# Two capacities swap ranks, the block sums change engine, and the next group's norm is taken one layer earlier

## The chip, the cores and the metric

The kernel runs on one core of a Trainium2 chip. The metric is the device time of one execution in microseconds (us). Its engines are named as the profile does: PE is TensorE (matmul) and PEld its weight load, DVE is VectorE, ACT is ScalarE, POOL is GpSimd, SP is the queue of SyncE that issues most DMA transfers.

## What is computed

Three blocks follow one another on 4608 tokens (8 batches of 576) of width 512:

```
scores = q k^T / 8 within chunks of 64 positions; attn = softmax(scores); x = attn v
e(t) = argmax of x[t] w_gate        (8 experts);  p(t) = its softmax probability
x[t] = p(t) * relu(x[t] w1[e]) w2[e]              (512 -> 1024 -> 512)
h = x w_in                                        (512 -> 2048)
g = h where h >= 1;  0 where h <= -1;  (h + 1)^2 / 4 between
out = g w_out                                     (2048 -> 512)
```

All inputs are float32 (w_in and w_out of the last block may be wider), drawn from a fixed seed. The sizes of the experts are thus data of the run: how many tokens choose each expert.

## The kernel before, in words

Every operand of a product is scaled by a power of two and split into a float16 high and a float16 low part (`high` on ScalarE, `low` on VectorE), and a product is three float16 products: high-high, high-low, low-high.

**Attention** runs over 36 tiles of 128 tokens. Behind it the tokens of each expert are listed in DRAM. **The expert stage** goes through eight slots r = 0 to 7. `RANKS[r]` says which expert a slot takes: the one of that rank when the experts are sorted by their number of tokens. Slot 0 is an exception: it takes the expert that has most tokens in the first 12 tiles, found early so that its weights can be loaded (`rank_first`), and this expert counts as rank 0 in the sorting (line 687). `CAPS[r]` is the number of tokens that slot r has room for; a slot over 512 is worked in two windows, of 384 and of the rest (line 743). Slot 2 has rank 1.

Tokens beyond a slot's capacity go through **the overflow loop** (`overflow`, lines 938 to 1069), a loop on the device whose number of trips is computed from the counts (`overflow_plan`: the tokens over each capacity in blocks of 128, and one more term that is zero unless slot 0 was misjudged). One trip loads the expert's weights again, scales and splits them, works 128 tokens, stores them, and then prepares the rows of group 0 of the next stage again (`again`).

**The last MLP** goes through nine groups of 512 tokens. Both layers are one level of Strassen-like block products: seven products in place of eight, on sums and differences of blocks. `rows_of(g)` prepares the first layer's operand: four loads from the expert outputs `yts` into `xf` by SP; eight squares with row sums on ScalarE, whose outputs go into the operand buffer `xt2` as junk; a maximum over the partitions on GpSimd (`allmax`, line 372); the power-of-two scale (`pow2`) on VectorE; four block differences (`B_SUMS`) on GpSimd (line 1168); then the high and low parts into `xt2`, and constants of the group (`mlp_consts`). `first_layer` (line 1218) makes for each of four column blocks jj seven products into PSUM (line 1232), sums between them (`add`, helper line 345), the activation (`gate`: ScalarE line 1242, VectorE lines 1247 and 1248, helper line 348), the splits of four operands (`split`: ScalarE line 1190, VectorE helper line 345), and four block sums S1 to S4 on GpSimd (line 1271) with their splits. `second_layer` (line 1276) makes seven products on these operands (line 1283), copies between PSUM banks (`copy`, line 1213), and scatters the output rows from GpSimd's queue (line 392).

**The order of the work** is written by a planner in the kernel (`Plan.order`): each operation is a task with an estimated duration (`cost`), tasks get due times backwards from TensorE's order, and an engine takes, of the tasks that are ready, the one due first. Each engine then executes its queue strictly in that order. For the last stage (`plan.beside`) the planner lengthens VectorE operations with two inputs in SBUF by 1.4 (tensor_tensor) or 1.22. In the trace the helpers' operations have the helper's line: 345 (`both`), 348 (`fused`), 375 (`square`), 378 (`high`), 381 (`low`).

Of the kernel before, what the change touches and what calls it, by code (L numbers as in the profile page):

```python
# [30 lines left out]
CAPS = (704, 512, 672, 480, 640, 448, 640, 672)  # L31
# [26 lines left out]
    KB * n for n in (0, 16, 32, 48, 76, 86, 92, 100, 108, 124, 131, 135, 179, 193, 201))  # L58
YS = [KB * n for n in (124, 126, 128, 193, 195, 197, 199)]
# [30 lines left out]
class Plan:  # L90
# [6 lines left out]
    def __init__(self, joined):  # L97
        self.tasks, self.writer, self.readers, self.joiners = [], {}, {}, {}
        self.clock, self.last = 0.0, None
        self.seen, self.joined, self.rows, self.beside, self.chains, self.links, self.direct = None, joined, set(), False, {}, set(), False  # L100
# [30 lines left out]
    def cost(self, engine, op, out, a, k):  # L131
# [12 lines left out]
        if engine == "DVE":  # L144
# [4 lines left out]
            if self.beside and n >= 256 and op != "tensor_scalar":  # L149
                apart = [v.space for v in [k.get(i) for i in ("in0", "in1")] if v is not None]  # L150
                if PSUM not in apart and len(apart) == 2:
                    t *= 1.4 if op == "tensor_tensor" else 1.22
# [141 lines left out]
def build(ctx, tc, qT, kT, v1, wg, w1, w2, wi, wo, out):  # L294
# [859 lines left out]
    def rows_of(g, eng):  # L1154
# [5 lines left out]
        for n in range(8):  # L1160
            t, c = n // 4, n % 4 * 64
            square(ss[:, n:n + 1], xf[:, 2 * t:2 * t + 2, :, c:c + 64], xt2[:, t, 0:2, :, c:c + 64].bitcast(BF16))
# [3 lines left out]
        for c0, c1 in (0, 1), (1, 2), (2, 3), (3, 4), (4, 5), (5, 7):  # L1166
            for o, x, y in {2: B_SUMS[:1], 3: B_SUMS[1:2], 4: B_SUMS[2:3], 5: B_SUMS[3:]}.get(c0, ()):
                do(lambda o=o, x=x, y=y: eng.tensor_tensor(out=xf[:, o], in0=xf[:, x], in1=xf[:, y], op=ALU.subtract))  # L1168
# [3 lines left out]
        mlp_consts(i_y, sets[g % 2])  # L1172
# [45 lines left out]
    def first_layer(g, ci):  # L1218
# [31 lines left out]
        for jj in range(4):  # L1250
# [19 lines left out]
            for o, a, b, f in (S1, A21, A22, ALU.add), (S2, S1, A11, ALU.subtract), (S3, A11, A21, ALU.subtract), (S4, A12, S2, ALU.subtract):  # L1270
                do(lambda o=o, a=a, b=b, f=f, jj=jj: pool.tensor_tensor(out=o.raw(jj), in0=a.raw(jj), in1=b.raw(jj), op=f))  # L1271
# [83 lines left out]
    for r in range(E):  # L1355
# [6 lines left out]
        while w < len(windows) and windows[w][0] == r:  # L1362
# [13 lines left out]
            if w == len(windows) - 2:  # L1376
# [3 lines left out]
                plan.beside = True  # L1380
                rows_of(0, pool)
                plan.beside = False
# [11 lines left out]
    overflow(lambda: rows_of(0, pool), [xf, xt2] + list(sets[0].values()))  # L1394

    plan.beside = True
    for g in range(NG):
        ci = sets[g % 2]
        first_layer(g, ci)
        if g + 1 < NG:  # L1400
            rows_of(g + 1, pool)
        second_layer(g, ci["io"])
# [59 lines left out]
```

## Time and profile before

| | |
|---|---|
| median of 3 timed runs | 1469.31 us (1461.74 to 1470.01) |
| profiled execution | 1454.82 us, of which the span from first to last instruction is 1453.1 us |
| mean granted TensorE clock | 0.939 |
| HBM read, written | 178.04 MB, 43.95 MB |

The timed runs and the profiled one are different executions. Busy time is the time in which an engine executes; "idle before" is the gap ahead of an instruction, with what ended it. An arrow out<-in names the buffers written and read; nearly all of SBUF is one tile, `arena`, and all PSUM banks are `psum`.

### The profile page before, as it was taken

To read this page: it belongs to the slowest core of one execution; us is meant where nothing else is said; L and a number is where in the kernel's file an instruction comes from. 1 tells how busy PE (TensorE), PEld (TensorE's weight loads), DVE (VectorE), ACT (ScalarE), POOL (GpSimd) and SP (SyncE) were. 2 spreads that over 40 slices of the span, in tenths; PEclk is the share of its full clock that TensorE was granted. 3 is DMA by queue.
4 is the path that set the end of the run, shared out by engine and by line. 5 is a ranking of instruction groups with operands and counts; after the bars stand their busy time and mean duration, and the time that the engine had idled before them with its cause. 6 is when DMAs were issued, how large, how long until landed. Compare 5 with 4: busy or idle time off the path is not lost.

```text
span 1453.1 us, 27496 instructions
## 1 busy us (share of the span) xinstructions
PE 1254.1 (86%) x10617; PEld 982.0 (68%) x10617; DVE 1035.7 (71%) x1977; ACT 852.3 (59%) x1550; POOL 513.8 (35%) x449
## 2 busy tenths in 40 slices
PE   6999695999999998532798998898998989899997
PEld 5777454557466575422687777787887778788776
DVE  5667477887787884222695968879595977969593
ACT  3444567887988883323564737565464736556462
POOL 3023143177211111110271625445261624527053
PEclk9999788999999999755899999999999999999998
DMA  9999558889989889231433517061442507053220
GB/s 231 288 259 250 165 201 198 271 226 288 271 216 252 273 242 310 97 66 37 135 98 104 159 32 216 15 218 45 136 127 75 187 2 233 29 159 103 91 92 30
DMA packets 149845, 233.50 MB, mean 161 GB/s; under 512 B 58111, under 2 KB 89343, under 8 KB 147665
## 3 DMA queue, kind: packets, MB, share of 16 engines
q1 hardware_dynamic: 139776, 207.95, 48.5%
q0 software_dynamic: 9936, 23.79, 5.8%
q8 instruction: 83, 1.36, 0.4%
q14 instruction: 50, 0.40, 0.1%
HBM read 178.04 MB, written 43.95 MB: 153 GB/s over the span
## 4 chain that ended last, share of the span: by engine, by line
PE 40%; DVE 29%; DMA 10%; issue 8%; ACT 7%; POOL 5%; SPq 1%; POOLq 0%; DVEq 0%; ACTq 0%
DVE arena L348 12%; DVE arena L345 12%; PE psum L1283 10%; PE psum L886 9%; PE psum L902 9%; PE psum L1232 6%; DMA arena<-arena 3%; POOL arena L1271 2%; DVE psum L345 2%; DMA arena<-kT 2%; PE psum L575 2%; PE psum L561 1%; PE psum L555 1%; DVE arena L381 1%; DMA yt<-arena 1%
## 5 line engine op out<-in xcount | busy, mean ns | idle before, releaser
L1232 PE MATMUL psum<-arena 128*128 128x256 f16 x3024 | 339.8, 273 | 58.1 <-DVE cells L345 28.3
L1283 PE MATMUL psum<-arena 128*128 128x256 f16 x3024 | 353.3, 279 | 30.1 <-ACT psum L1213 26.4
L1232 PEld LDWEIGHTS <-arena 128*128 128x128 f16 x3024 | 296.3, 98 | 98.7 <-issue 64.2
L1283 PEld LDWEIGHTS <-arena 128*128 128x128 f16 x3024 | 302.3, 100 | 75.4 <-issue 27.8
L1271 POOL TENSOR_TENSOR arena<-arena 128x512 f32<-128x512 f32 x144 | 229.4, 1608 | 191.6 <-DVE arena L348 172.6
L345 DVE TENSOR_TENSOR arena<-arena 128x512 f16<-128x512 f32 (+5 forms) x301 | 266.8, 915 | 15.9 <-ACT arena L1190 13.9
L1190 ACT ACTIVATE arena<-arena 128x512 f16<-128x512 f32 x252 | 154.6, 627 | 124.3 <-DVE arena L345 56.6
L886 PE MATMUL psum<-arena 128*128 128x384 f16 (+6 forms) x1248 | 205.1, 327 | 20.6 <-DMA arena<-arena 14.6
L381 DVE SCALAR_TENSOR_TENSOR arena<-arena,cells 128x1024 f16<-128x1024 f32 (+2 forms) x186 | 190.6, 1062 | 29.0 <-ACT arena L378 27.2
L378 ACT ACTIVATE arena<-arena,cells 128x1024 f16<-128x1024 f32 (+2 forms) x186 | 168.8, 960 | 65.0 <-DVE cells L342 37.4
L902 PE MATMUL psum<-arena 128*128 128x384 f16 (+6 forms) x1248 | 198.2, 319 | 2.9 <-ACT arena L891 1.0
L886 PEld LDWEIGHTS <-arena 128*128 128x128 f16 x1248 | 124.8, 100 | 97.7 <-issue 23.6
L348 DVE SCALAR_TENSOR_TENSOR arena<-psum,cells,arena 128x512 f32<-128x512 f32 x171 | 125.4, 747 | 81.0 <-PE psum L1283 43.4
L902 PEld LDWEIGHTS <-arena 128*128 128x128 f16 x1248 | 121.8, 98 | 76.3 <-issue 2.7
L348 DVE SCALAR_TENSOR_TENSOR arena<-arena,cells 128x512 f32<-128x512 f32 x108 | 132.4, 1232 | 44.3 <-ACT arena L1242 44.1
L1242 ACT ACTIVATE arena<-psum,cells 128x512 f32<-128x512 f32 x144 | 107.4, 771 | 40.8 <-DVE psum L345 20.1
L375 ACT ACTIVATE arena<-arena 128x1024 bf16<-128x1024 f32 (+1 forms) x160 | 115.7, 727 | 10.0 <-DMA arena<-yt 7.5
L392 POOL DMA_INDIRECT out<-arena,sid x36 | 40.6, 1128 | 186.7 <-DVE arena L348 150.5
L372 POOL PARTITION_ALL_REDUCE cells<-cells x47 | 21.4, 456 | 235.2 <-DVE cells L351 157.8
L392 POOL DMA_INDIRECT ld<-arena x36 | 35.1, 974 | 119.1 <-DVE arena L612 50.1
L1168 POOL TENSOR_TENSOR arena<-arena 128x512 f32<-128x512 f32 x40 | 63.6, 1598 | 33.9 <-issue 16.5
L892 DVE SCALAR_TENSOR_TENSOR arena<-psum,arena 128x384 f16<-128x384 f32 (+6 forms) x104 | 54.8, 536 | 27.8 <-ACT arena L891 27.4
(189 smaller groups left out, 1165.6 us busy)
## 6 DMA issues: line engine op xcount, KB each, us to landing
arena<-wd SPq DMA_DIRECT2D x252, 256.0 KB, 3.1
arena<-w SPq DMA_DIRECT2D x64, 512.0 KB, 7.3
arena<-yt SPq DMA_DIRECT2D x40, 256.0 KB, 4.8
arena<-v SPq DMA_DIRECT2D x36, 260.0 KB, 7.3
xd<-arena SPq DMA_DIRECT2D x18, 512.0 KB, 7.3
arena<-qT SPq DMA_DIRECT2D x16, 512.0 KB, 11.1
arena<-kT SPq DMA_DIRECT2D x32, 256.0 KB, 8.5
arena<-w_in SPq DMA_DIRECT2D x8, 1024.0 KB, 5.5
```

The source lines that it names most:

```text
L345: do(lambda: dve.tensor_tensor(out=out, in0=a, in1=b, op=op))
L348: do(lambda: dve.scalar_tensor_tensor(out=out, in0=a, scalar=s, in1=b, op0=op, op1=op1))
L375: do(lambda: act.activation(out=junk, in_=src, func=AF.Square, scale=scale, accum_out=ss))
L378: do(lambda: act.activation(out=hi, in_=src, func=AF.Copy, scale=s))
L381: do(lambda: dve.scalar_tensor_tensor(out=lo, in0=src, scalar=s, in1=hi, op0=ALU.mult, op1=ALU.subtract))
L886: pe.matmul(h[:, 0:n], lhsT=wa[:, a, wc:wc + P], rhs=xt[:, 4 * b + dc, 0:n], start=dc == 0 and i == 0, stop=dc == 3 and i == 2)
L902: pe.matmul(ybanks[db][:, 0:n], lhsT=wb[:, b, f * D + db * P:f * D + db * P + P], rhs=ht[:, a, f, 0:n], start=f == 0 and i == 0, stop=f == ...
L1190: do(lambda: act.activation(out=self.parts(0, jj), in_=self.raw(jj), func=AF.Copy))
L1232: pe.matmul(banks[to][:, k], lhsT=w[:, k, x, dc * P:(dc + 1) * P], rhs=xt2[:, z, b, dc], start=start and (k, dc, m) == (0, 0, 0), stop=(k, ...
L1242: do(lambda: act.activation(out=r, in_=at[src], func=AF.Relu, scale=a, bias=b))
L1271: do(lambda o=o, a=a, b=b, f=f, jj=jj: pool.tensor_tensor(out=o.raw(jj), in0=a.raw(jj), in1=b.raw(jj), op=f))
L1283: pe.matmul(banks[to][:, i], lhsT=a.part(x, j, i * P, P), rhs=wot[b][:, j, v], start=start and (j, i, n) == (0, 0, 0), stop=(j, i, n) == ( ...
```

## The change

The capacities of slots 0 and 2 are exchanged. The four block differences of `rows_of` and the four block sums of `first_layer` are issued on VectorE (`both`) in place of GpSimd. `rows_of` becomes two functions: `load_rows` has the loads, squares, maximum, scale, differences and constants, `split_rows` the high and low parts. For group g + 1 the first is called ahead of group g's first layer, the second stays between the layers. The squares' outputs go to a buffer of their own (`junk`). The planner's lengthening for work beside GpSimd is removed.

```diff
--- before.py
+++ after.py
@@ -28,7 +28,7 @@
 BIG = 1 << 20
 LC = NT + 4
 RANKS = (0, 5, 1, 6, 3, 7, 4, 2)
-CAPS = (704, 512, 672, 480, 640, 448, 640, 672)
+CAPS = (672, 512, 704, 480, 640, 448, 640, 672)
 WIDE = 384
 BATCH = (6, 6, 6, 4, 6, 5, 3)
 GB = max(BATCH)
@@ -56,6 +56,7 @@
 KB = 1024
 WT0, WT1, WT2, RAWS, XG, XH, XT0, XT1, HT, Y, NU, STAGE, RINGS, FREE, END = (
     KB * n for n in (0, 16, 32, 48, 76, 86, 92, 100, 108, 124, 131, 135, 179, 193, 201))
+JUNK = 134 * KB
 YS = [KB * n for n in (124, 126, 128, 193, 195, 197, 199)]
 XF, XT = 135 * KB, 149 * KB
 OPS = [KB * n for n in (0, 72, 82, 32, 92, 102, 112)]
@@ -97,7 +98,7 @@
     def __init__(self, joined):
         self.tasks, self.writer, self.readers, self.joiners = [], {}, {}, {}
         self.clock, self.last = 0.0, None
-        self.seen, self.joined, self.rows, self.beside, self.chains, self.links, self.direct = None, joined, set(), False, {}, set(), False
+        self.seen, self.joined, self.rows, self.chains, self.links, self.direct = None, joined, set(), {}, set(), False
 
     def keys(self, ap):
 
@@ -146,10 +147,6 @@
                 return 0.1 + 0.0003 * n
             t = max(0.15, 0.12 + (0.0006 if op == "tensor_scalar" and n > 64 and out.space != PSUM else 0.00112) * n)
             t += 0.05 * (op == "scalar_tensor_tensor" and n > 64)
-            if self.beside and n >= 256 and op != "tensor_scalar":
-                apart = [v.space for v in [k.get(i) for i in ("in0", "in1")] if v is not None]
-                if PSUM not in apart and len(apart) == 2:
-                    t *= 1.4 if op == "tensor_tensor" else 1.22
             return t
         if engine == "POOL":
             return {"indirect_dma_start": 1.27, "partition_all_reduce": 0.4, "tensor_tensor": 0.2 + 0.0027 * n}.get(op, 0.4)
@@ -1151,7 +1148,9 @@
     xt2 = view(XT, (2, 7, 2, HD), F16)
     wot = [view(a, (8, 2, HD), F16) for a in WOT]
 
-    def rows_of(g, eng):
+    junk = [view(JUNK + 512 * i, (2, 2, 64), BF16) for i in range(2)]
+
+    def load_rows(g):
 
         for db in range(4):
             dh, dc = divmod(db, 2)
@@ -1159,17 +1158,20 @@
         ss, am, ag = cell(8), cell(), cell()
         for n in range(8):
             t, c = n // 4, n % 4 * 64
-            square(ss[:, n:n + 1], xf[:, 2 * t:2 * t + 2, :, c:c + 64], xt2[:, t, 0:2, :, c:c + 64].bitcast(BF16))
+            square(ss[:, n:n + 1], xf[:, 2 * t:2 * t + 2, :, c:c + 64], junk[n % 2])
         reduce(am, ss, ALU.max)
         allmax(ag, am)
         s, i_y = pow2(ag, TY, 1, True)
-        for c0, c1 in (0, 1), (1, 2), (2, 3), (3, 4), (4, 5), (5, 7):
-            for o, x, y in {2: B_SUMS[:1], 3: B_SUMS[1:2], 4: B_SUMS[2:3], 5: B_SUMS[3:]}.get(c0, ()):
-                do(lambda o=o, x=x, y=y: eng.tensor_tensor(out=xf[:, o], in0=xf[:, x], in1=xf[:, y], op=ALU.subtract))
+        for o, x, y in B_SUMS:
+            both(xf[:, o], xf[:, x], xf[:, y], ALU.subtract)
+        mlp_consts(i_y, sets[g % 2])
+        return s
+
+    def split_rows(s):
+
         for c0, c1 in (0, 2), (3, 4), (4, 5), (2, 3), (5, 7):
             high(xt2[:, 0, c0:c1], xf[:, c0:c1], s)
             low(xt2[:, 1, c0:c1], xt2[:, 0, c0:c1], xf[:, c0:c1], s)
-        mlp_consts(i_y, sets[g % 2])
 
     class Operand:
 
@@ -1268,7 +1270,7 @@
             gate(z, A21, jj, 1)
             A22.split(jj)
             for o, a, b, f in (S1, A21, A22, ALU.add), (S2, S1, A11, ALU.subtract), (S3, A11, A21, ALU.subtract), (S4, A12, S2, ALU.subtract):
-                do(lambda o=o, a=a, b=b, f=f, jj=jj: pool.tensor_tensor(out=o.raw(jj), in0=a.raw(jj), in1=b.raw(jj), op=f))
+                both(o.raw(jj), a.raw(jj), b.raw(jj), f)
             A12.split(jj)
             for o in S2, S1, S3, S4:
                 o.split(jj)
@@ -1377,9 +1379,7 @@
                 for n in (0, 6, 1, 5, 4, 2, 3):
                     for j in 0, 4:
                         do(lambda n=n, j=j: sp.dma_start(out=wot[n][:, j:j + 4].rearrange("p a x c -> p (a x c)"), in_=wdo[n][:, j:j + 4].rearrange("p j c -> p (j c)")))
-                plan.beside = True
-                rows_of(0, pool)
-                plan.beside = False
+                split_rows(load_rows(0))
                 for n in range(RING):
                     fetch_unit(n)
             gt = cell()
@@ -1391,14 +1391,14 @@
             if w == 2:
                 overflow_plan()
             w += 1
-    overflow(lambda: rows_of(0, pool), [xf, xt2] + list(sets[0].values()))
-
-    plan.beside = True
+    overflow(lambda: split_rows(load_rows(0)), [xf, xt2] + junk + list(sets[0].values()))
+
     for g in range(NG):
         ci = sets[g % 2]
+        s = load_rows(g + 1) if g + 1 < NG else None
         first_layer(g, ci)
         if g + 1 < NG:
-            rows_of(g + 1, pool)
+            split_rows(s)
         second_layer(g, ci["io"])
 
     E_ = mybir.EngineType
```

## Rows read from the trace of the kernel before

**Rows 1.** The page, part 1: busy time and share of the span by engine.
```profile
PE 1254.1 (86%) x10617; PEld 982.0 (68%) x10617; DVE 1035.7 (71%) x1977; ACT 852.3 (59%) x1550; POOL 513.8 (35%) x449
```

**Rows 2.** Busy time by stretch: from:to, length, engines, PE clock, DMA share, GB/s.
```profile
0.00:603.80 603.80, 548.52 (x4377) 365.45 (x4377) 428.11 (x1099) 400.69 (x737) 172.43 (x213) 0.96 0.83 239
603.80:698.60 94.80, 21.00 (x193) 17.92 (x192) 24.61 (x67) 30.49 (x61) 15.90 (x16) 0.56 0.23 63
866.30:948.20 81.90, 74.39 (x675) 65.67 (x674) 65.28 (x93) 47.65 (x87) 36.96 (x25) 1.00 0.38 117
```

**Rows 3.** Timeline around the overflow loop (start, length, instruction, idle before), and one group.
```profile
593.95 0.23 DVE L983 TENSOR_SCALAR loop<-csum,jt 128x10 f32<-128x10 f32 x1 [0.59 <-DVE arena L892]
603.52 0.38 PE L898 MATMUL psum<-arena 128*128 128x512 f16 x1
...
L1052 PE MATMUL psum<-arena 128*128 128x128 f16 x96 | 11.5, 308 | 34.8 <-DMA arena<-arena 29.9 <-DVE arena L1055 4.8
...
698.61 26.35 PE L1232 MATMUL psum<-arena 128*128 128x256 f16 x228 [28.29 <-DVE cells L345]
```

**Rows 4.** Timeline of TensorE alone in the last MLP's groups.
```profile
768.55 12.96 PE L1283 MATMUL psum<-arena 128*128 128x256 f16 x102 [3.64 <-ACT psum L1213]
903.98 2.78 PE L1232 MATMUL psum<-arena 128*128 128x256 f16 x24 [1.71 <-DVE psum L345]
935.08 11.29 PE L1283 MATMUL psum<-arena 128*128 128x256 f16 x102 [3.19 <-ACT psum L1213]
1350.72 14.16 PE L1283 MATMUL psum<-arena 128*128 128x256 f16 x102 [3.12 <-ACT psum L1213]
1408.90 34.22 PE L1283 MATMUL psum<-arena 128*128 128x256 f16 x312
```

**Rows 5.** Groups by line and shape: busy, mean ns, idle before with releasers.
```profile
L1283 PE MATMUL psum<-arena 128*128 128x256 f16 x3024 | 353.3, 279 | 30.1 <-ACT psum L1213 26.4 <-DVE arena L345 3.7
L1232 PE MATMUL psum<-arena 128*128 128x256 f16 x3024 | 339.8, 273 | 58.1 <-DVE cells L345 28.3 <-DVE psum L345 25.2 <-DVE arena L348 4.5
L345 DVE TENSOR_TENSOR arena<-arena 128x512 f16<-128x512 f32 x252 | 241.7, 993 | 15.1 <-ACT arena L1190 13.9
L1271 POOL TENSOR_TENSOR arena<-arena 128x512 f32<-128x512 f32 x144 | 229.4, 1608 | 191.6 <-DVE arena L348 172.6 <-DVE psum L345 15.2
L348 DVE SCALAR_TENSOR_TENSOR arena<-arena,cells 128x512 f32<-128x512 f32 x108 | 132.4, 1232 | 44.3 <-ACT arena L1242 44.1
L1168 POOL TENSOR_TENSOR arena<-arena 128x512 f32<-128x512 f32 x40 | 63.6, 1598 | 33.9 <-issue 16.5 <-DMA arena<-yt 15.9
L345 DVE TENSOR_TENSOR arena<-arena 128x512 f32<-128x512 f32 x32 | 21.9, 687 | 0.4
```

**Rows 6.** Timeline ahead of the copy of line 1213 in one group.
```profile
929.01 0.15 DVE L351 TENSOR_REDUCE cells<-cells 128x1 f32<-128x8 f32 x1
932.04 0.38 POOL L372 PARTITION_ALL_REDUCE cells<-cells  x1 [5.91 <-issue]
933.39 1.15 ACT L378 ACTIVATE arena<-arena,cells 128x1024 f16<-128x1024 f32 x1 [2.91 <-DVE cells L342]
934.45 0.58 ACT L1213 ACTIVATE psum<-psum 128x512 f32<-128x512 f32 x1
```

**Rows 7.** Timeline while the rows of group 0 are prepared, end of the expert stage.
```profile
560.72 0.16 DVE L351 TENSOR_REDUCE cells<-cells 128x1 f32<-128x8 f32 x1 [4.23 <-ACT arena L375]
568.73 0.38 POOL L372 PARTITION_ALL_REDUCE cells<-cells  x1 [8.65 <-issue]
578.57 1.25 POOL L1168 TENSOR_TENSOR arena<-arena 128x512 f32<-128x512 f32 x1 [9.46 <-issue]
582.83 8.13 PE L886 MATMUL psum<-arena 128*128 128x288 f16 x42 [5.98 <-DVE arena L892]
```

**Rows 8.** Timeline of single VectorE operations, before and after GpSimd's first block sum.
```profile
707.80 0.69 DVE L345 TENSOR_TENSOR arena<-arena 128x512 f16<-128x512 f32 x1 [0.94 <-ACT arena L1190]
710.75 0.75 DVE L348 SCALAR_TENSOR_TENSOR arena<-arena,cells 128x512 f32<-128x512 f32 x1 [1.65 <-ACT arena L1242]
713.43 6.43 POOL L1271 TENSOR_TENSOR arena<-arena 128x512 f32<-128x512 f32 x4 [19.73 <-DVE arena L348]
908.44 1.75 DVE L348 SCALAR_TENSOR_TENSOR arena<-arena,cells 128x512 f32<-128x512 f32 x1
```

## The prediction

> **What bounds the kernel now.** I read the page's busy shares first [rows 1]: TensorE is busy 86% of the span, VectorE 71%, GpSimd 35%. Such averages hide stages, so the stage table came next [rows 2]: three stretches show three machines. Up to 603.8 us TensorE is busy 91% of the time. From 603.8 to 698.6 us it is busy 21 of 94.8 us, at a granted clock far below full, and the DMA engines are busy 23% against 83% before. After that nine groups of the last MLP follow; the one shown has TensorE busy 74 of 82 us and VectorE 65.
>
> The timeline says what the hole is [rows 3]. The last matmul before it ends at 603.90 (603.52 + 0.38), the first one of group 0 starts at 698.61, and between them run lines 983 to 1066, the body of the overflow loop: its matmul line L1052 ran 96 times in the program, 8 x 12, which is one trip. The trip is there because an expert has more tokens than its slot has room. Counted with the reference's own functions on its inputs, the experts get 621, 452, 649, 506, 688, 417, 657 and 618 tokens. Expert 2 has most of the first twelve tiles (357 of 1536) and so takes slot 0, rank 0, with 649; the largest of the others, expert 4 with 688, is rank 1 and takes slot 2, whose capacity is 672. It overflows by 16 tokens: one block, one trip.
>
> In the groups I read TensorE's own timeline [rows 4]. In the last group, which has no next one to prepare, TensorE streams 312 second-layer matmuls in 34.22 us, 0.1097 us each; 672 of them are 73.7 us. The wait that every group but the last shows ends at 768.55 first and at 1350.72 for the eighth time, so the period is 582.17 / 7 = 83.2 us, and 9.5 us of a group are lost. The group table of TensorE's two lines splits it [rows 5]. The second layer waits 26.4 us for the copy of line 1213 (once in each of the 8 groups with a next one: 3.3 us) and 3.7 us for splits (0.46). The first layer, without the 28.3 us of the hole, waits 25.2 + 4.5 us for sums and gates on VectorE, 3.3 us in each of 9 groups. [...]
>
> What the 3.3 us wait is made of is the most useful reading here [rows 6]. The copy Y1 <- X1 needs nothing from the next group, but it stands on ScalarE's queue behind a high part of the next group's rows (L378, 1.15 us), which waits for the scale, which waits for the all-reduce on GpSimd: the reduce of the squares is done at 929.16, GpSimd starts on it only at 932.04, and the copy ends at 935.03. GpSimd had sat 5.9 us on "issue" after its last block sum. The same pair of operations shows 8.65 and 9.46 us of issue when the rows of group 0 are prepared [rows 7].
>
> **The change, part by part.** Sums are against the profiled execution, 1454.8 us (span 1453.1 and 1.7 around it), which lies 14.5 us under the median of the timed runs, 1469.3.
>
> The swap of capacities. Slot 0 gets 672 for 649 tokens, slot 2 gets 704 for 688: no slot overflows, the loop runs no trip. It takes away 94.7 us between the two matmuls. What stays is the empty loop: each engine reads the count, compares and jumps, and the first layer must start. No row shows a loop without a trip. The lower bound is VectorE's way into it, 0.59 us [rows 3]; the upper is the longest issue gap near by, 9.5 us [rows 7]. I take 5, between them: the weights and rows of group 0 are in place by then, but the engines must come out of the loop and the last stores must land. Gain 89.7 us, bounds 85 to 94. [...] The windows keep their number, 320 + 288 columns swap places in slots 0 and 2, and their matmuls are as many: nothing.
>
> The rows of group 0 (line 1381). Their four differences leave GpSimd for VectorE. VectorE waits 4.2 us in this stretch before the reduce alone, so four operations of 0.687 us [rows 5, 7] cost nothing. TensorE's wait of 5.98 us at 582.83 comes after two issue gaps on GpSimd, ScalarE being held at a high part [rows 7]. I take 4 us of gain; bounds 0 (a store holds ScalarE as well) and 6.
>
> The block sums in the groups. GpSimd loses 16 + 4 sums of 1.6 us per group [rows 5] and keeps one all-reduce and four scatters. VectorE gains 20 of 0.687 us, 13.7 us. It also loses the lengthening that it shows while GpSimd sums: the split's difference takes 0.993 us on average against 0.69 alone, and the product of line 1247 (helper line 348) takes 1.232 against 0.75 [rows 5, 8]. Over a group that is 28 x 0.30 + 12 x 0.48 = 14.2 us. So VectorE's load stays at 65 us, and its chains get shorter: a block sum takes 0.69 instead of 1.6 us, and no queue on GpSimd lies between. [...]
>
> How much of the first layer's 3.3 us goes? The longest, 1.71 us, comes late in the first layer [rows 4], when VectorE has no idle time. Its load there is about the same after, but the planner's costs for it (line 147) are now close to the rows (0.69 and 0.74 us at 512 columns), while the removed factors of 1.4 and 1.22 stood for durations that scatter from 0.69 to 1.75 us [rows 8]. I take half, 1.65 us; bounds -1.5 and 3.3.
>
> The norm ahead. Eight squares with their read-outs, the reduce, the all-reduce, scale, differences and constants move into the first layer of the group before; their four loads on SP move with them, and the row buffer is free from the start of the group, so no engine's queue is held by them (DMA share 0.38 [rows 2]). ScalarE's busy share is 47.6 of 82 us, and the squares no longer wait for slots of the operand buffer. The high parts find their scale ready, so the copy goes out on time. Behind the moved all-reduce on VectorE's queue stands the scale's first step; were it planned too early, gates would wait 2 to 3 us, which is the lower bound above. Gain 3.3 + 0.46 + 1.85 = 5.6 us in each of 8 groups; late next is VectorE's own run of sums and splits, some 65 us of the 76.
>
> The sum: 5.6 + 1.65 = 7.3 us x 8 = 58, and 1.65 in the last group: 60. With 89.7 and 4 it is 154, so 1301 us on the profiled level. The timed runs lie 7 to 15 us above that level; I add 8 and forecast **1309 us**, a period near 76 us.
>
> **Rivals.**
> TensorE alone bounds the groups (12%): all 9.3 us of waits and clock go, 8 x 9.3 + 3.3 = 78 us, and the time is 1454.8 - 89.7 - 4 - 78 + 8 = 1291. For it: the last group streams its second layer without a wait. Against: in the fourth block no other product is left to fill in.
>
> The groups gain nothing (14%): VectorE's 13.7 us take the place of the lengthening and the wait only moves to a sum; 1454.8 - 94 + 8 = 1369. For it: the first layer's waits are for VectorE already [rows 5]. Against: the longest wait is for a scale [rows 6], not for VectorE's load.
>
> VectorE becomes the bound (3%), the slower side: the lengthening is not GpSimd's doing and stays, the sums add in series, 9 x 13.7 = 123 us against 94 gained, 1454.8 + 29 + 8 = 1492. It decides from 10.4 us a group on. Against it, the same operations take 0.75 us before 713.4, when GpSimd has not begun, and 1.75 after [rows 8]. [...]
>
> The swap does nothing (3%), if the chip's ranks or counts differ from mine so that some slot still overflows: 1454.8 - 60 - 4 + 8 = 1399. Against it: one trip, as counted [rows 3].
>
> **The numbers.** The forecast has 68%. Its bounds run from 1277 (94, 6 and 78 us gained, nothing added) to 1347 (85, 0 and 8 x 4.1 - 1.5 = 31 gained, 8 added); with the 12% of the second case, 1280 to 1345 holds 8 in 10 and leaves out the rest. A change of 1%, some 15 us, is about the least that can be told here. Only the 3% of the VectorE case are slower by that, and something between is worth 2%: faster 0.95.
>
> **What would show it.** Right: no L1005 or L1052 in the trace, a gap of 1 to 10 us before the first L1232; no GpSimd TENSOR_TENSOR; the split's difference near 0.69 us and line 1247's near 0.75; no wait of 3 us for line 1213, the period near 76. Wrong: a trip still there; a period of 80 or more with waits for line 345; a clock that falls elsewhere.

## The result and the profile after

The changed kernel takes 1299.26 us (median of 4 runs, 1296.84 to 1307.92) against 1469.66 (4 runs): a ratio of 0.8861, 95% interval 0.8808 to 0.8914. The forecast was 1309, with 1280 to 1345 as its range. The profiled execution of the changed kernel was its longest, 1307.92 us; that of the kernel before, 1454.82, was its shortest, which matters below. In the changed kernel the helpers stand three lines higher (345 is now 342, 348 is 345, 351 is 348, 372 is 369, 378 is 375), and the two matmul lines of the groups are 1234 and 1285.

Busy time and share by engine, from the page's first part, to be held against [rows 1]:

```profile
PE 1226.1 (94%) x10425; PEld 960.7 (74%) x10425; DVE 984.7 (75%) x2067; ACT 820.6 (63%) x1490; POOL 202.8 (16%) x251
```

TensorE is now busy 94% of the span. VectorE has 90 instructions more and yet 51 us less of busy time. Half of that is the trip's own work, 24.6 us in the hole [rows 2]; the other half, 25 us in the groups, is the first sign that its instructions became shorter. The table by stretch (from:to, length, then PE, PEld, DVE, ACT, POOL busy, PE clock, DMA share, GB/s), as in [rows 2]: expert stage, the gap, one group:

```profile
0.00:623.00 623.00, 559.96 (x4377) 368.62 (x4377) 426.94 (x1080) 401.65 (x737) 160.63 (x207) 0.95 0.80 231
623.00:628.80 5.80, 0.08 (x1) 0.00 (x0) 0.00 (x0) 0.44 (x1) 0.00 (x0) 0.75 0.25 73
779.42:853.34 73.92, 73.81 (x674) 65.72 (x672) 63.09 (x113) 47.31 (x87) 4.80 (x5) 1.00 0.42 129
```

The hole of 94.8 us is 5.8 us, and a group is 73.92 us, of which TensorE works 73.81. VectorE's 63 us in it hold 113 instructions where 93 took 65 us before. TensorE's own timeline of the gap and of one group, against [rows 3, 4]:

```profile
622.71 0.38 PE L895 MATMUL psum<-arena 128*128 128x512 f16 x1
628.83 11.35 PE L1234 MATMUL psum<-arena 128*128 128x256 f16 x85 [5.75 <-issue]
...
779.42 33.39 PE L1234 MATMUL psum<-arena 128*128 128x256 f16 x300
812.65 1.47 PE L1285 MATMUL psum<-arena 128*128 128x256 f16 x12
814.05 4.09 PE L1234 MATMUL psum<-arena 128*128 128x256 f16 x36
817.97 35.53 PE L1285 MATMUL psum<-arena 128*128 128x256 f16 x324
```

No row of the group has an idle time behind it, and lines 1005 and 1052 (the trip of the overflow loop) are gone from the trace. The groups by line and shape, against [rows 5]:

```profile
L1234 PE MATMUL psum<-arena 128*128 128x256 f16 x3024 | 338.2, 273 | 7.9 <-issue 5.7 <-DMA arena<-wd 0.7 <-DVE psum L342 0.7
L1285 PE MATMUL psum<-arena 128*128 128x256 f16 x3024 | 333.2, 273 | 0.0
...
L342 DVE TENSOR_TENSOR arena<-arena 128x512 f16<-128x512 f32 x252 | 163.8, 686 | 0.4 <-ACT arena L1192 0.3
L342 DVE TENSOR_TENSOR arena<-arena 128x512 f32<-128x512 f32 x212 | 143.8, 687 | 39.1 <-DMA arena<-yt 37.3
...
L345 DVE SCALAR_TENSOR_TENSOR arena<-arena,cells 128x512 f32<-128x512 f32 x108 | 80.7, 747 | 11.2 <-ACT arena L1244 10.1 <-issue 0.6
```

The waits of TensorE, 30.1 us on the second layer's line and 58.1 on the first layer's before (28.3 of them the hole), are 0.0 and 7.9, of which 5.7 are the gap. The split's difference went from 993 to 686 ns, the product from 1,232 to 747. Last, the rows of group 0, against [rows 7] (and [rows 6], the same chain in a group): reduce, all-reduce, high parts.

```profile
587.68 0.16 DVE L348 TENSOR_REDUCE cells<-cells 128x1 f32<-128x8 f32 x1 [1.72 <-ACT arena L372]
...
587.93 0.72 POOL L369 PARTITION_ALL_REDUCE cells<-cells  x1 [19.48 <-DVE cells L348]
...
590.14 4.03 ACT L375 ACTIVATE arena<-arena,cells 128x1024 f16<-128x1024 f32 x5 [2.03 <-DVE cells L339]
```

The all-reduce starts 0.09 us after the end of the reduce (587.93 against 587.84). Before, 2.88 us lay between them in the group of [rows 6], and 7.85 at group 0 [rows 7]. TensorE's 5.98 us wait in this stretch is gone.

So far the account of the two profiles is: expert stage 19.2 us longer (its last matmul ends at 623.09 against 603.90), hole 89.0 shorter, and from the first matmul of group 0 to the end 677.1 us in place of 754.5, 77.4 shorter. Together 147.2, the difference of the spans. Three questions are left: which of the two moves in the groups made the 77, what GpSimd had to do with it, and why the expert stage is longer.

### The profile page after: what moved, and what is told of

Same layout as the page of the kernel before. It is cut to its first block, busy times and chain, and to the rows that moved or that the text cites. A ratio compares the mean times of both kernels' runs of the same rounds, so it can differ in the third digit from the quotient of the medians.

```text
span 1305.9 us, 26744 instructions
## 1 busy us (share of the span) xinstructions
PE 1226.1 (94%) x10425; PEld 960.7 (74%) x10425; DVE 984.7 (75%) x2067; ACT 820.6 (63%) x1490; POOL 202.8 (16%) x251
## 4 chain that ended last, share of the span: by engine, by line
PE 45%; DVE 4%; ACT 1%; issue 1%; DMA 1%; POOL 0%; POOLq 0%; SPq 0%; DVEq 0%
PE psum L1285 25%; PE psum L1234 20%; DVE arena L345 2%; DVE arena L342 1%; DVE psum L342 1%; DMA arena<-wd 1%; ACT arena L1244 1%; POOL out L389 0%; ACT arena L1246 0%; ACT arena L1192 0%; DVE cells L337 0%; POOLq L1427 0%; ACT psum L1215 0%; ACT arena L1215 0%; ACT arena L372 0%
## 5 line engine op out<-in xcount | busy, mean ns | idle before, releaser
L1234 PE MATMUL psum<-arena 128*128 128x256 f16 x3024 | 338.2, 273 | 7.9 <-issue 5.7
L1285 PE MATMUL psum<-arena 128*128 128x256 f16 x3024 | 333.2, 273 | 0.0
L342 DVE TENSOR_TENSOR arena<-arena 128x512 f16<-128x512 f32 (+4 forms) x481 | 299.7, 669 | 42.3 <-DMA arena<-yt 37.3
L378 DVE SCALAR_TENSOR_TENSOR arena<-arena,cells 128x1024 f16<-128x1024 f32 (+2 forms) x181 | 184.1, 1061 | 11.4 <-ACT arena L375 10.5
L389 POOL DMA_INDIRECT out<-arena,sid x36 | 36.5, 1013 | 600.1 <-DVE arena L345 539.6
L1244 ACT ACTIVATE arena<-psum,cells 128x512 f32<-128x512 f32 x144 | 106.9, 769 | 29.5 <-DVE psum L342 21.4
L345 DVE SCALAR_TENSOR_TENSOR arena<-arena,cells 128x512 f32<-128x512 f32 x108 | 80.7, 747 | 11.2 <-ACT arena L1244 10.1
L888 ACT ACTIVATE arena<-psum 128x384 f16<-128x384 f32 (+6 forms) x104 | 48.1, 471 | 60.3 <-PE psum L883 35.5
L1215 ACT ACTIVATE arena<-psum,cells 128x512 f32<-128x512 f32 x27 | 18.4, 682 | 84.6 <-PE psum L1285 68.4
L1215 ACT ACTIVATE psum<-psum 128x512 f32<-128x512 f32 x54 | 31.4, 582 | 57.3 <-PE psum L1234 35.4
L369 POOL PARTITION_ALL_REDUCE cells<-cells x46 | 24.6, 536 | 273.8 <-DVE cells L348 243.0
```

The source lines that it names most:

```text
L342: do(lambda: dve.tensor_tensor(out=out, in0=a, in1=b, op=op))
L345: do(lambda: dve.scalar_tensor_tensor(out=out, in0=a, scalar=s, in1=b, op0=op, op1=op1))
L378: do(lambda: dve.scalar_tensor_tensor(out=lo, in0=src, scalar=s, in1=hi, op0=ALU.mult, op1=ALU.subtract))
L1234: pe.matmul(banks[to][:, k], lhsT=w[:, k, x, dc * P:(dc + 1) * P], rhs=xt2[:, z, b, dc], start=start and (k, dc, m) == (0, 0, 0), stop=(k, ...
L1244: do(lambda: act.activation(out=r, in_=at[src], func=AF.Relu, scale=a, bias=b))
L1285: pe.matmul(banks[to][:, i], lhsT=a.part(x, j, i * P, P), rhs=wot[b][:, j, v], start=start and (j, i, n) == (0, 0, 0), stop=(j, i, n) == ( ...
```

## The experiments

Three theories of the groups were held against each other. The forecast's own: the norm taken ahead is worth 5.6 us a group, the moved sums 1.65. The first rival: the sums alone do it, because GpSimd's work lengthens VectorE's. The second: it is the order in which the planner now issues, since its lengthening factors are gone. The medians of the kernel before are 1469.17 us for the first four runs, 1472.19 for e7, e8, e12 and e13, and 1479.23 for e9, e10, e11 and e14; across these, ratios are compared.

**e1_caps: the swap alone.**

```
-CAPS = (704, 512, 672, 480, 640, 448, 640, 672)
+CAPS = (672, 512, 704, 480, 640, 448, 640, 672)
```

> The kernel before with the two capacities swapped and nothing else. Forecast's theory: no overflow trip, so the hole of 94.7 us between the expert stage and group 0 shrinks to about 6 us (the kernel after has 5.7), and nothing in the groups moves: period 83 us, ratio (1469.7 - 89) / 1469.7 = 0.939. Rival (the trip also hides something that shows once it is gone, as loads or code for the groups): gain under 80 us, ratio over 0.946. Rival (the 19 us later end of the expert stage in the kernel after, 623.1 against 603.9, comes with the swap: 320 columns in slot 2): the expert stage ends near 620 here too, ratio near 0.95.

Measured: 1379.81 us (1366.39 to 1389.15), ratio 0.9401 [0.9342, 0.9460]. The last expert matmul ends at 614.82 and the gap is 5.72 us, to 620.54. In the groups TensorE's waits and VectorE's durations are as before (groups by line, from 620 us on):

```profile
L1283 PE MATMUL psum<-arena 128*128 128x256 f16 x3024 | 345.7, 276 | 29.2 <-ACT psum L1213 25.5 <-DVE arena L345 3.7
L1232 PE MATMUL psum<-arena 128*128 128x256 f16 x3024 | 340.0, 273 | 34.6 <-DVE psum L345 25.2 <-issue 5.7 <-DVE arena L348 3.3
...
L345 DVE TENSOR_TENSOR arena<-arena 128x512 f16<-128x512 f32 x252 | 241.8, 993 | 14.7 <-ACT arena L1190 13.5
L348 DVE SCALAR_TENSOR_TENSOR arena<-arena,cells 128x512 f32<-128x512 f32 x108 | 131.3, 1222 | 60.3 <-ACT arena L1242 58.7 <-issue 1.5
```

The swap is worth 0.06 of 1469, 88 us, and nothing of the groups' waits goes with it. These four runs lie 23 us apart, so how much belongs to the swap and how much to the sums below is known to some 10 us only.

**e2_caps_sums: the swap, and all block sums on VectorE; the norm stays between the layers.** The planner's factors go too.

```
-  do(lambda ...: eng.tensor_tensor(out=xf[:, o], in0=xf[:, x], in1=xf[:, y], op=ALU.subtract))
+  both(xf[:, o], xf[:, x], xf[:, y], ALU.subtract)
-  do(lambda ...: pool.tensor_tensor(out=o.raw(jj), in0=a.raw(jj), in1=b.raw(jj), op=f))
+  both(o.raw(jj), a.raw(jj), b.raw(jj), f)
-  plan.beside = True
```

> Swap, and all block sums on VectorE with the planner's lengthening removed; the next group's norm stays between the layers, its squares' junk in the operand buffer. Forecast's theory: the first layer's waits fall by half and the all-reduce follows its reduce at once, but the copy of line 1213 still stands behind a high part that waits for the scale: period 77 to 80 us, ratio 0.90 to 0.92. Rival (the waits were all VectorE's lengthened load and GpSimd's switching between sums and all-reduce, the place of the norm is worth nothing): period 74 to 75, ratio as the kernel after, 0.886.

Measured: 1302.57 us (1299.01 to 1307.08), ratio 0.8863 [0.8823, 0.8903]: the whole effect of the change, without the norm ahead. The period is 73.92 us. The chain that held up the copy before [rows 6], here in the timeline of one group, with the norm still between the layers:

```profile
752.93 0.15 DVE L351 TENSOR_REDUCE cells<-cells 128x1 f32<-128x8 f32 x1
...
753.18 1.31 POOL L372 PARTITION_ALL_REDUCE cells<-cells  x1 [45.19 <-DVE cells L351]
...
755.48 1.15 ACT L378 ACTIVATE arena<-arena,cells 128x1024 f16<-128x1024 f32 x1 [1.13 <-DVE cells L342]
756.53 0.58 ACT L1213 ACTIVATE psum<-psum 128x512 f32<-128x512 f32 x1
```

The high part still stands ahead of the copy and still waits for the scale, but from the start of the reduce to the start of the copy it takes 3.60 us where it took 5.44 (929.01 to 934.45), since GpSimd begins at once. That is 1.84 us, and the wait that went was 3.19 [rows 4]. The rest is that the reduce itself comes earlier: by the matmul rows, after some 180 of the second layer's 336 products, where it came after some 203. TensorE doesn't stand still for the copy any more.

**e3_caps_norm: the swap, and the norm ahead; sums on GpSimd, planner's factors kept.**

```
 (the changed kernel, with the two sums' lines as before)
-  both(o.raw(jj), a.raw(jj), b.raw(jj), f)
+  do(lambda ...: pool.tensor_tensor(out=o.raw(jj), in0=a.raw(jj), in1=b.raw(jj), op=f))
```

> Swap, and the next group's norm one layer earlier; all block sums stay on GpSimd, and the planner keeps its lengthening. Forecast's theory: the 3.3 us wait for the copy, the 0.46 and most of the slow clock behind it go, the first layer's 3.3 us stay: period 77 to 78 us, ratio 0.905 to 0.915. Rival (VectorE's load is what counts): VectorE stays lengthened, 65 us busy, period 80 to 83, ratio 0.92 to 0.94.

Measured: 1399.16 us (1391.17 to 1406.56), ratio 0.9528 [0.9480, 0.9576]: 19 us slower than the swap alone. The wait for the copy did go (TensorE's second-layer line has 0.0 us idle), but a new one came. VectorE's, GpSimd's and TensorE's timelines in one group (here VectorE's helpers are lines 341, 346 and 352, the all-reduce 373, the sums 1170 and 1277, the first layer 1238):

```profile
884.01 0.16 DVE L352 TENSOR_REDUCE cells<-cells 128x1 f32<-128x8 f32 x1 [2.43 <-ACT arena L376]
889.63 0.34 DVE L341 TENSOR_SCALAR cells<-cells 128x1 int32<-128x1 int32 x2 [5.46 <-POOL cells L373]
...
889.23 0.38 POOL L373 PARTITION_ALL_REDUCE cells<-cells  x1 [6.38 <-issue]
896.89 2.49 POOL L1170 TENSOR_TENSOR arena<-arena 128x512 f32<-128x512 f32 x2 [7.29 <-issue]
...
890.92 2.02 PE L1238 MATMUL psum<-arena 128*128 128x256 f16 x12 [2.52 <-DVE cells L341]
894.52 19.12 PE L1238 MATMUL psum<-arena 128*128 128x256 f16 x156 [1.57 <-DVE psum L346]
```

GpSimd needs 6.38 us of "issue" before the all-reduce and 7.29 before the next sum. With the norm between the layers ScalarE stood there; with the norm ahead VectorE does, at the scale's first step, with the gates queued behind it. The forecast had named this wait, at 2 to 3 us and as its lower bound for the sums; it is 5.46. Neither expectation came true, since both (0.905 to 0.94) made this kernel at least as fast as the swap alone.

**e4_after_again: the changed kernel, once more**, so that e2 has it beside it.

> The kernel after, unchanged, for another profile of it. If the later end of its expert stage (623.1 against 603.9 us, with TensorE waiting on issue between 327 and 373 us while slot 2 is worked) belongs to one execution, this profile has it earlier, near 600, and a span near 1290; if it belongs to the kernel, it shows again at the same place. Ratio 0.886 either way; period 73.9 us.

Measured: 1303.94 us (1297.49 to 1318.35), ratio 0.8897 [0.8836, 0.8957], against 0.8863 for e2. No worth of the norm ahead can be told. The last expert matmul ends at 610.72, between the two values that the expectation held against each other (623.1 and 600), so this profile alone does not settle why the expert stage is longer; e9 below does more.

**e8_old_costs: e2 with the planner's factors kept** (`plan.beside = True` stays).

> All sums on VectorE, norm in its old place, ranks swapped, with the old factors in the planner's costs (1.4 and 1.22 for VectorE's operations of two inputs from SBUF) kept, so that only the order of issue can differ. If the order that the new costs give had part in the gain, this is slower than 1315 us with a period over 75 us. If the engines' own times made it, 1297 to 1308 us and a period of 73.9 us.

Measured: 1305.02 us (1298.76 to 1307.63), ratio 0.8868 [0.8812, 0.8923]. No part of the planner's order can be told.

**e7_rows_on_pool and e12_ops_on_pool: e2 with a part of the sums on GpSimd**, the four of the rows or the sixteen of the first layer.

```
 e7:   do(lambda ...: eng.tensor_tensor(out=xf[:, o], ...))        # as before
 e12:  do(lambda ...: pool.tensor_tensor(out=o.raw(jj), ...))      # as before
```

> The two ranks swapped and the first layer's sums on VectorE, norm and scale in their old place, but the block sums of the rows (4 of the 20 in a group) on GpSimd as before. Theory 'the norm's chain': GpSimd's change between sums and all-reduce, some 6 us each, stands ahead of the next group's first product and makes most of the 9.3 us per group; then the period is 78 to 81 us, TensorE waits again for a copy, and the time is 1340 to 1365 us. Theory 'the first layer': the 16 sums of the gates lengthen VectorE's operations while TensorE waits for VectorE; then 4 sums elsewhere cost little: period 74 to 75.5 us, 1303 to 1318 us, and VectorE's operations stay under 760 ns.

Measured: 1319.43 us (1312.08 to 1323.70), ratio 0.8978 [0.8929, 0.9027]: four sums a group on GpSimd cost 17 us by the medians, 7 in the profiled stretch of the groups, and the period is 75.1 us (777.38 to 852.48). TensorE's wait at the rows of group 0 is back too, with 5.52 us. The time is 1 us over what the second theory allowed, and the product of line 1247 takes 793 ns, not under 760, but the copy's wait is absent. GpSimd alternates its two kinds of work here as well, yet its last sum ends 19 us ahead of the all-reduce, which then starts 0.14 us after its reduce (761.49):

```profile
761.63 1.31 POOL L372 PARTITION_ALL_REDUCE cells<-cells  x1 [19.36 <-DVE cells L351]
```

> The other half: ranks swapped and the rows' block sums on VectorE, the first layer's 16 sums per group on GpSimd as before. Theory 'the norm's chain': the all-reduce still follows sums on GpSimd, so some 6 us stay ahead of it in each group, but the rows' own sums no longer wait for a second change: period 76 to 79 us, 1320 to 1345 us. Theory 'the first layer': the whole loss comes back, VectorE's operations at 990 and 1,230 ns, period 81 to 83 us, 1365 to 1385 us. If only both together cost the 9.3 us, each half alone is under 1320 us.

Measured: 1393.20 us (1390.46 to 1396.46), ratio 0.9477 [0.9424, 0.9530], the means at 1,005 and 1,093 ns: the first layer's sixteen bring the whole loss back, and a little more than e1 has or the expectation gave. The wait for the copy comes back with them, without any sum of the rows on GpSimd, since the first layer's last sum ends at 760.33, just ahead of the all-reduce. The reduce is done at 762.76 (the wait is put down to a later operation of VectorE). TensorE's second layer from 615 us on, and that all-reduce:

```profile
L1283 PE MATMUL psum<-arena 128*128 128x256 f16 x3024 | 349.1, 279 | 20.4 <-ACT psum L1213 20.4
...
766.21 0.38 POOL L372 PARTITION_ALL_REDUCE cells<-cells  x1 [5.88 <-DVE arena L345]
```

(e1 also has the planner's factors; which of the two differences makes the rest wasn't tried.)

**e13_spare_sums and e14_spare_spread: e2, and sixteen sums a group on GpSimd that nothing reads.** They add a small zeroed bfloat16 buffer to itself; the kernel's own work is unchanged. In e14 each is tied behind the VectorE sum of its place. In these two kernels line 1234 is the first layer's product, 1286 the second's and 1274 the useless sum.

```
   both(o.raw(jj), a.raw(jj), b.raw(jj), f)
+  do(lambda: pool.tensor_tensor(out=spare, in0=spare, in1=spare, op=ALU.add))                                # e13
+  do(lambda: pool.tensor_tensor(out=spare, in0=spare, in1=spare, op=ALU.add), after=len(plan.tasks) - 1)     # e14
```

> All sums on VectorE, norm in its old place, ranks swapped, and 16 sums per group on GpSimd that nothing reads (512 bfloat16 numbers each, in place), issued where the first layer's sums were. Theory 'two engines at one memory': VectorE's operations lengthen though nobody waits for GpSimd, from 690 and 750 ns towards 990 and 1,230, and the period grows to 77 us or more, 1330 us or more. Theory 'waiting for GpSimd': what cost the time was that VectorE and ACT waited for GpSimd's sums (each 1.6 us against 0.75); then VectorE's operations stay under 780 ns and the time within 1300 to 1315 us, unless GpSimd's change ahead of the all-reduce shows as a wait of 5 us or more on the all-reduce, which would give 1330 to 1350 us.

Measured: 1391.14 us (1384.92 to 1393.50), ratio 0.9444 [0.9388, 0.9499]. Tied to nothing, the sums all came early: 48 ahead of group 0's first product, the last by 877 us. The expert stage ended 61 us later than in e2 (675.04 against 614.37), which is most of the 89 us between the two: there all-reduces and useless sums alternate on GpSimd, with 5.93 to 8.49 us of "issue" at each change from 600 us on. The time as a whole thus says little about the theory. A marker that comes once a group, in TensorE's timeline, shows the rest:

```profile
726.06 1.47 PE L1286 MATMUL psum<-arena 128*128 128x256 f16 x12
...
813.24 1.47 PE L1286 MATMUL psum<-arena 128*128 128x256 f16 x12
...
895.80 1.47 PE L1286 MATMUL psum<-arena 128*128 128x256 f16 x12
...
970.86 1.47 PE L1286 MATMUL psum<-arena 128*128 128x256 f16 x12
...
1044.78 1.47 PE L1286 MATMUL psum<-arena 128*128 128x256 f16 x12
```

Between the marks lie 87.2, 82.6, 75.1 and 73.9 us: slow while the useless sums run, at full speed once they are over, in one execution.

> All sums on VectorE, norm in its old place, ranks swapped, and 16 sums per group on GpSimd that nothing reads (512 bfloat16 numbers each, in place), each tied behind the VectorE sum of the same place, so that they are spread over all groups; in the run before they all came early, and the groups that had 40 of them took 83 to 87 us against 73.9 without. Theory 'two engines at one memory': every group has VectorE operations lengthened in part (the spare sums take 1.26 us each, 20 us of 74), TensorE waits for VectorE in the first layer, period 76 to 80 us, 1320 to 1355 us. Theory 'the waits for GpSimd's results': period 73.9 to 74.5 us and 1300 to 1310 us, since nobody waits for these sums.

Measured: 1355.89 us (1349.11 to 1370.66), ratio 0.9197 [0.9108, 0.9287], a period of 80.2 us, both just above the first theory's ranges. In one group, TensorE's, GpSimd's and VectorE's timelines:

```profile
775.00 17.19 PE L1234 MATMUL psum<-arena 128*128 128x256 f16 x156
793.03 2.78 PE L1234 MATMUL psum<-arena 128*128 128x256 f16 x24 [0.84 <-DVE psum L345]
798.82 7.07 PE L1234 MATMUL psum<-arena 128*128 128x256 f16 x48 [3.00 <-DVE psum L345]
806.90 8.10 PE L1234 MATMUL psum<-arena 128*128 128x256 f16 x72 [1.01 <-DVE psum L345]
...
789.32 16.96 POOL L1274 TENSOR_TENSOR arena<-arena 128x512 bf16<-128x512 bf16 x12
...
794.52 3.63 DVE L345 TENSOR_TENSOR arena<-arena 128x512 f32<-128x512 f32 x3
798.08 0.69 DVE L345 TENSOR_TENSOR psum<-psum,arena 128x512 f32<-128x512 f32 x1
...
800.97 1.52 DVE L348 SCALAR_TENSOR_TENSOR arena<-arena,cells 128x512 f32<-128x512 f32 x1
802.52 0.75 DVE L348 SCALAR_TENSOR_TENSOR arena<-psum,cells,arena 128x512 f32<-128x512 f32 x1
...
806.75 0.74 DVE L348 SCALAR_TENSOR_TENSOR arena<-arena,cells 128x512 f32<-128x512 f32 x1
...
809.45 1.28 DVE L345 TENSOR_TENSOR arena<-arena 128x512 f32<-128x512 f32 x2
```

GpSimd is busy from 789.32 to 806.28, and TensorE's three waits fall where that stretch makes VectorE late. In the rows shown a sum of two SBUF operands takes 1.21 us within it and a product 1.52; after it, 0.64 (1.28 for two) and 0.74. Not every one is lengthened: a split at 803.19 takes 0.74. An operation with one operand in PSUM takes 0.69 or 0.75 throughout. Over the groups VectorE's busy time tells the same; the stretch is the first group's start to the end, of e14 and then of e2:

```profile
617.20:1347.10 729.90, 678.87 (x6048) 597.50 (x6048) 631.03 (x987) 423.61 (x753) 241.75 (x188) 0.98 0.38 114
```

```profile
620.45:1297.90 677.45, 665.54 (x6048) 591.84 (x6048) 559.12 (x987) 419.38 (x753) 45.58 (x44) 0.99 0.40 123
```

The same 987 instructions take 71.9 us longer, and the stretch 52.4 us longer, because of work on which nobody waits. The useless sums are shorter than the real ones (1.41 us against 1.61 [rows 5]), so 52 us is no upper bound of what this does before. How the other 15 to 25 us of the sums' worth divide between the real sums' own length and GpSimd's change ahead of the all-reduce was not separated. Of the operations of 512 columns in these rows only those with two SBUF operands are longer, and so they are over the groups, e14 against e2: the split's difference takes 750 ns on average against 684 and the product 922 against 746, where operations of the same two kinds with an operand in PSUM take 691 against 692 and 747 against 748. Whether such an operation stands still until GpSimd's sum ends or is only slowed, these rows don't tell: by an estimate from them, a wait for the rest of a GpSimd sum of 1.41 us (16.96 for twelve) would give between 0.69 and 2.1 us, and 1.21 and 1.52 lie within that.

From the first matmul of group 0 to the end, in all profiles (us; e9 to e11 are told below):

| kernel | sums on | norm | stretch |
|---|---|---|---|
| before; again (e9) | GpSimd | between | 754.5; 746.2 |
| e1 | GpSimd | between | 744.2 |
| e3 | GpSimd | ahead | 762.5 |
| e12 | 16 GpSimd, 4 VectorE | between | 773.7 |
| e7 | 4 GpSimd, 16 VectorE | between | 684.5 |
| e2; e8; e10; e11 | VectorE | between | 677.5; 679.5; 677.5; 677.9 |
| after; again (e4) | VectorE | ahead | 677.1; 678.9 |
| e14 | VectorE, and 16 useless on GpSimd | between | 729.9 |
| e13 | VectorE, and 144 useless, early | between | 706.7 |

**e9_before_again: the kernel before, unchanged**, for its expert stage.

> The kernel before once more, for its expert stage: its profiled execution was its fastest. If the 54.7 us of slot 2's stretch were chance, this profile shows 60 us or more there and its last expert matmul ends at 607 to 615 us; if they belong to the capacities' old order, it shows 53 to 57 us again and 602 to 606 us. The groups' period is 83 us in either case.

Measured: 1476.84 us (8 runs, 1467.99 to 1479.85), ratio 0.9973 [0.9940, 1.0005]; its profile has a span of 1477.7 us. Both expectations were too low: the last expert matmul ends at 635.51. Slot 2's stretch, from its first matmul to slot 3's, in the table by stretch, of the profile before and of this one:

```profile
302.80:357.50 54.70, 54.70 (x386) 37.55 (x385) 44.24 (x88) 44.28 (x82) 43.38 (x42) 1.00 0.90 254
```

```profile
321.80:391.20 69.40, 61.28 (x386) 38.66 (x385) 44.30 (x88) 44.41 (x82) 43.42 (x42) 0.93 0.79 211
```

The same 386 matmuls take 54.7 us in one execution and 69.4 in another of the same kernel, and the first expert window starts at 181.82 in one and 198.75 in the other. The stage after needs no explanation by the swap: it ends at 609 to 623 us in the nine profiles with the swap (e13 with its useless sums left aside), and the two of the kernel before lie on both sides of that. The profile before is the odd one, with the earliest first window of all profiles and the only slot 2 under 66 us.

**e10_both_704: e2 with 704 places in slot 0 and in slot 2.**

```
+CAPS = (704, 512, 704, 480, 640, 448, 640, 672)
```

> All sums on VectorE, norm in its old place, and 704 places in both slot 0 and slot 2 (neither overflows). If slot 2's stretch of 66 to 68 us in the kernels with swapped ranks comes from its second window being 320 wide, it is 66 us or more here too, and the time 1303 to 1312 us. If it comes from slot 0 being 32 places shorter (its work ends earlier, the next weights are not there), it is 57 us here and the time 1293 to 1302 us.

Measured: 1302.48 us (1301.50 to 1304.56), ratio 0.8807 [0.8750, 0.8863]; slot 2 takes 67.4 us. By the expectation's letter that speaks for the 320 columns, but e9 has 69.4 with 288, so neither theory holds: it is 66 to 76 us in every profile but that of the kernel before. What holds TensorE there, mostly "issue" in its timeline, wasn't settled.

**e11_tight: e2 with each capacity cut towards the counts.**

```
+CAPS = (656, 512, 688, 464, 624, 432, 624, 672)
```

> All sums on VectorE, norm in its old place, and each capacity the next multiple of 16 (two of slots 1 and 7 unchanged): 656, 512, 688, 464, 624, 432, 624, 672, in all 96 places fewer than with the swap. If the expert stage is bound by what each place costs on TensorE (2.6 us for 32 places at slot 2's rate), 1292 to 1298 us. If its stretches are set by loads of weights or by VectorE and ScalarE, no change: 1299 to 1308 us.

Measured: 1290.44 us (1289.12 to 1292.20), ratio 0.8725 [0.8669, 0.8781], all its runs below all of e10's on the same chip, and 2 us below the range expected. It has 128 places fewer than e10, and its expert stage ends 13 us earlier in the profile (603.84 against 616.83). It is the fastest version here, for these counts; a seed with other counts would overflow sooner.

## Why the prediction was right, and which step failed

**The swap: right.** Forecast 89.7 us with a gap of 5; measured a gap of 5.74 us in place of 94.7 in the profiles, and 88 us by e1. The empty loop's price, for which no row stood before, is 5.7 to 6.2 us in the profiles without a trip, nearly all of it "issue" (9.0 in e13, where GpSimd was busy with its useless sums until 681.55).

**Rows of group 0: right.** Forecast 4 us; the wait that went measured 5.98, 5.16, 5.71, 5.52 and 5.68 us in the five profiles that have the rows' differences on GpSimd (before, e1, e3, e7, e9), and is absent in those that have them on VectorE, but for e13 with its useless sums.

**The norm ahead, 5.6 us in each of 8 groups: wrong, this is the step that failed.** The chain [rows 6] was read rightly up to its last link: copy behind high part, behind scale, behind all-reduce, behind 5.91 us of GpSimd's "issue". The forecast then let the norm's place remove the wait, and left the issue time as given. But the issue time belongs to GpSimd's change from a sum to an all-reduce. With no sums it is gone (0.10 us from reduce to all-reduce in e2), the copy is on time wherever the norm stands, and no difference of e2 and e4 can be told. It is also harmless where the last sum lies far enough ahead (e7), and the wait is back where the first layer's sums stand right before the all-reduce (e12). With the sums kept, the norm ahead only hands the same 6 us to VectorE, and costs 19 us (e3). The 1.85 us in the 5.6 are shown by no run as a cost of the wait: the three stretches of 102 matmuls in [rows 4], each behind a wait, ran at granted clocks of 0.87, 1.00 and 0.79, and in e2, where no wait stands ahead of the second layer, 324 matmuls take 35.53 us, 0.1097 each.

**The sums, 1.65 us a group: wrong in size.** They took all that TensorE had lost: 77 us by the medians (1379.81 to 1302.57), 67 by the two profiled stretches (744.2 to 677.5), where the forecast gave them 15 and both moves together 60. "I take half" rested on the planner's costs and the scatter of durations; e8 shows the costs to be worth nothing. The estimate of 14.2 us of lengthening in a group was sound: the 811 instructions of before took 582.98 us in the stretch, 176 more at 0.687 would make 703.9, and 557.80 were measured after, 16.2 us a group less. What was missed is that this slack lay just where TensorE waited. e14 gives its price by itself, 52 us of stretch.

**The rivals.** "TensorE alone bounds the groups" (12%, 1291) is what happened: nearly all waits went, the groups' granted clock is 0.99 where it was 0.97 (their 6,048 matmuls keep TensorE busy for 666.09 us in place of 684.57), the period is 73.92 us, and 672 x 0.1097 is 73.7. Its 78 us compare with 77.4 in the profiles (the terms that it lists come to 8.9 us a group, not 9.3, and so to 75). Its reason against, that no product is left to fill in in the fourth block, did not hold once VectorE's operations were short. "The groups gain nothing" and "VectorE becomes the bound" fell with e2, "the swap does nothing" with e1.

**The basis.** The forecast of 1309 came near 1299 with a gain in the groups too small by 17 us by the medians (7 by the profiles) and a basis too low by 7: 1454.8 + 8 = 1462.8 us, where the kernel before measured 1469.66 beside the kernel after (and 1469 to 1479 later). The two errors partly cancel, so the nearness is in part luck. Against e9 the profiled execution before is ahead by 17 us before the first expert window, where e9 is the latest of all profiles, and by 15 us in slot 2, where the profile before stands alone.

## What to carry to other kernels

Where VectorE works near its limit and TensorE waits for it, count what GpSimd's elementwise work does to VectorE's two-operand instructions before you count what it saves: here 144 sums took 229 us on GpSimd [rows 5] and would take 99 on VectorE (0.687 us each), yet VectorE got less busy in the groups when it took them over (582.98 to 557.80 us). If an engine shows several us of "issue" between two kinds of operation (5.8 to 9.5 here), remove one kind, or leave time between the two, rather than move the work that waits. And when a chain has a wait to explain, ask of each link whether the edit beside it removes it too, or two edits will be credited with one gain.

## What the runs showed of the hardware

From the end of an elementwise sum on GpSimd to the start of a partition all-reduce behind it, the eight groups before show 5.84 to 6.35 us, and in e12 GpSimd is idle for 5.89 us on average ahead of its eight in the groups. With both orders, and where nothing else was awaited, 5.8 to 9.5 us show as "issue" ([rows 6, 7]; 6.38 behind a scatter that follows the sums, and 7.29 behind the all-reduce, in e3; 7.05 and 7.28 behind the all-reduce in e14). The time runs from the end of the earlier operation: in the last such group before, an instruction MODIFY_POOL_CONFIG of the all-reduce's line stands at 1342.1, right behind the sum that ends at 1341.85 and ahead of the reduce at 1344.73, and the all-reduce starts at 1347.69; in e7 the all-reduce 19 us behind its sum shows no "issue". In e2 GpSimd has no such sums, and the all-reduce follows its reduce by 0.10 us.

A device loop that makes no trip leaves TensorE idle for 5.7 to 6.2 us (9.0 in e13). One kernel's executions differ by 32 us up to the end of the expert stage (603.90 and 635.51), while the groups behind it differ by 8 (754.5 and 746.2): a gain that lies in the steady part can be read from profiles, one before it needs many runs.
